# A virtual clock reckons the load of Gelu's table and longer loads of rows: a long convolution beside a gated MLP on one core

## The chip, the cores and the metric

The kernel runs on one core of a Trainium2 chip. The metric is the device time of one execution in microseconds; less is better. The number compared is the median of several runs.

## The reference

Everything is float32, with 2048 tokens of 576 features and a hidden width of 4608.

```python
def reference(A_u, ...):
    x = A_u
    xn = _layernorm(x, axis=-1)
    s = _A_ref(xn, ...)        # S4D: per feature a kernel of 2048 taps, K = 2 Re sum_n C exp(A dt l);
                               # y = irfft(rfft(xn) * rfft(K)) + xn * D_skip
    g = _silu(_B_ref(xn, ...)) # layernorm -> w1 + b1 -> tanh-approximated gelu -> w2 + b2
    return x + s * g
```

## The kernel before

The work on TensorE has two parts. The first is the MLP. It runs in 48 half-slots, counted from 0; each takes 3 x 128 hidden features (a group of `NG` = 12) and 512 of the tokens. A half-slot has three blocks of the first layer (L619, 14 matmuls each, 512 columns), and then eight units of the second layer (L682, 72 matmuls of 288 columns), which add to four row blocks j of the accumulator. Numbers are split into a high and a low part, so each hidden block passes through three steps: ScalarE's gelu (L655), ScalarE's copy to the high part `hh` (L658), VectorE's subtraction to the low part `hl` (L661). The first matmul that reads the third low part stands 18 matmuls and a bit behind the end of the third block. VectorE adds each finished row block to `acc` (L692). Weights are split the same way (L572 on ScalarE, L569 on VectorE).

The second part is the long convolution, in six chunks of 96 features. It is laid as "scan work" between the MLP's blocks on TensorE, in the two PSUM tiles named `cv`: table products (L996), first transforms (L1108, L1139), a second one (L1167), inverses (L1210, L1236). Its tables come from sines. For each of 36 table blocks VectorE forms phases (L917, L920), ScalarE rounds them (L923), VectorE takes the fraction (L926), ScalarE folds it (L929) and takes two sines (L934, L936), and VectorE weighs them by magnitudes (L942 forms the magnitudes; L951, L953, L955, L957 weigh). ScalarE holds one table at a time: gelu's and sine's differ, and plain copies run under either.

At the end the three factors are joined. For the first eight token blocks a combine loads rows of u, s and g into three of four `row` buffers (`combine_load`, L721 to L723, on GpSimd's queue), multiplies and adds on VectorE (L729, L730) and stores (L733). The other eight are finished behind the last two half-slots: ScalarE's tanh or silu (L765), VectorE's products and sum (L770, L772, L776, L780), and stores (L782).

The order in which all this is issued is fixed when the program is recorded. A class `Order` keeps a virtual clock for each engine and reckons a duration for each step (`act`, `dve` and the like). Between two units of TensorE, `advance` records every step of the side lines that is ready before TensorE's clock and that would end before the next step with a due time ("soon", in which gelus, low parts and additions stand) would have to begin. `take` adds 1.28 for a table load whenever a step's table isn't the current one. Ahead of a second-layer unit, `force` records the earliest startable steps, whatever they are, until that unit's inputs are recorded. A None step is a wait on the clock alone; in `end_line` one of 10 us stands for the landing of a combine's rows. `end_line` is started in half-slot 38 and its eleven combines follow each other: eight after the fourth chunk's rows are stored, and three after the last chunk's.

Of the kernel before, what the change touches and what calls it, by code (L numbers as in the profile page):

```python
# [19 lines left out]
NT = 16  # L20
# [19 lines left out]
def dve(n):  # L40
    return 0.075 + 0.00104 * n
# [10 lines left out]
class Order:  # L52
# [85 lines left out]
    def advance(self, horizon):  # L138
        while True:
            best = None  # L140
            soon = dict(self.next)
            for u in self.urgent:
                st = u[1][0]
                k = (max(u[0], self.t[st["eng"]]), 0)
                if u[0] <= horizon and (best is None or k < best[0]):
                    best = (k, u, None)
                for st in u[1]:
                    soon[st["eng"]] = min(soon.get(st["eng"], 1e9), st["by"])
            for x in self.lines:
                if x["steps"] and x["steps"][0]["by"] < 1e9:  # L150
                    st = x["steps"][0]
                    soon[st["eng"]] = min(soon.get(st["eng"], 1e9), max(st["by"], self.t[st["eng"]] + st["dur"]))
            for n, x in enumerate(self.lines):
                h = self.head(x)
                if h is None or h[0]["eng"] == "PE":
                    continue
                st, r = h
                if st["eng"] is None:
                    k = (max(r, 0), 1 + n)
                    if r > horizon:  # L160
                        continue
                else:
                    e = st["eng"]
                    b = max(self.t[e], r)
                    d = st["dur"]
                    if st["tbl"]:
                        d += 1.28 * (1 + (st["tbl"] != self.tbl))
                    if b > horizon or b + d > soon.get(e, 1e9) + st["late"]:
                        continue
                    k = (b, 1 + n)  # L170
                if best is None or k < best[0]:
                    best = (k, None, x)
            if best is None:
                break
            if best[1] is not None:
                self.go(best[1])
            else:
                self.run(best[2])
            self.pin()
# [26 lines left out]
def step(eng, dur, fn, need=(), mark=None, cv=0, at=0.0, late=0.0, tbl=None, by=1e9):  # L206
    return dict(eng=eng, dur=dur, fn=fn, need=tuple(need), mark=mark, cv=cv, at=at, late=late, tbl=tbl, by=by)
# [3 lines left out]
def mixer_kernel(ctx, tc, u, log_a_real, a_imag, c_real, c_imag, log_dt, d_skip, w1, b1, w2, b2,  # L211
# [506 lines left out]
    def combine_load(b, n, c0, c1):  # L718
        m = c1 - c0
        r = [sb.tile([P, D], F32, name="row", bufs=NROW)[:, :n * m].rearrange("p (i d) -> p i d", i=n) for _ in range(3)]  # L720
        nc.gpsimd.dma_start(r[0], u_s[:, b:b + n, c0:c1])  # L721
        nc.gpsimd.dma_start(r[1], s_s[:, b:b + n, c0:c1])
        nc.gpsimd.dma_start(r[2], g_s[b:b + n, :, c0:c1].rearrange("i p d -> p i d"))  # L723
        XS[b] = r

    def combine(b, n, c0, c1):

        x, s, g = XS[b]
        nc.vector.tensor_mul(s, s, g)  # L729
        nc.vector.tensor_add(x, x, s)  # L730
        for i in range(n):
            for y, o in enumerate(rows_at(out, b + i, c0, c1)):
                nc.gpsimd.dma_start(o, x[64 * y:64 * y + 64, i])  # L733
# [19 lines left out]
    def finish(b, c0, c1, silu, second_queue, z=None):  # L753

        c = slice(c0, c1)
        z = acc[:, b - 8, c] if z is None else z
        n = c1 - c0
        T = []

        def act_z():  # L760
            if n < D:
                T.append(sb.tile([P, TB], F32, name="h32", bufs=2)[:, :n])
            else:
                T.append(sb.tile([P, D], F32, name="row", bufs=NROW))
            nc.scalar.activation(T[0], z, AF.Silu if silu else AF.Tanh, scale=1.0 if silu else 0.5)  # L765

        def mul():
            s = XS[b][1][:, c]
            if silu:
                nc.vector.scalar_tensor_tensor(s, s, 2.0, T[0], op0=OP.mult, op1=OP.mult)  # L770
            else:
                nc.vector.tensor_mul(s, s, z)  # L772

        def mul2():
            s = XS[b][1][:, c]
            nc.vector.scalar_tensor_tensor(s, T[0], 1.0, s, op0=OP.add, op1=OP.mult)  # L776

        def total():
            x, s = XS[b]
            nc.vector.tensor_add(x[:, c], x[:, c], s[:, c])  # L780
            for y, o in enumerate(rows_at(out, b, c.start, c.stop)):
                (second_queue if y else nc.sync).dma_start(o, x[64 * y:64 * y + 64, c])  # L782
        st = [step("ACT", act(n), act_z, tbl="silu" if silu else "gelu"), step("DVE", dve(n), mul)]
        if not silu:
            st.append(step("DVE", dve(n), mul2))
        return st + [step("DVE", dve(n), total)]
# [485 lines left out]
    el, wl2, wl, nl2, pl, pl2, nl, ml, ml2, xl, wx, c3, c2, c1, c4, kl, tl, sl, vl, gl, odl, fl = [od.line() for _ in range(22)]  # L1272
# [181 lines left out]
    def wmark(n, which):  # L1454

        per = KB + 1 + G
        a = n * per + (0 if which == 1 else KB + 1)
        return [("w", k) for k in range(a, a + (KB + 1 if which == 1 else G))]
# [23 lines left out]
    for k in range(8):  # L1482
        gl["steps"].append(step("POOL", 0.7, lambda k=k: part.update({k: load_f2(k)}), mark=("f2", k),
                                need=[("f2c", k - 2)] if k > 1 else ["turns"]))
        fl["steps"].append(step(None, 4.5, lambda: None, need=[("f2", k)]))
        for f in range(2):
            fl["steps"].append(step("ACT", act(256), lambda k=k, f=f: part[k](f), mark=("f2c", k) if f else None,
                                    need=[("f2s", k - 1)] if k and k % 2 == 0 else []))
# [26 lines left out]
    def end_line():  # L1515
        for c, c0, c1, sets in ((NCH - 3, 0, CE, [(b, 1) for b in range(8)]), (NCH - 1, CE, D, [(0, 3), (3, 3), (6, 2)])):
            for b, n in sets:
                a = (b, n, c0, c1)
                ml["steps"].append(step(None, 10.0, lambda a=a: combine_load(*a), need=[("st", c), ("u", NT - 1)]))
                ml["steps"].append(step("DVE", 2 * dve(n * (c1 - c0)), lambda a=a: combine(*a)))  # L1520
                ml["steps"].append(step(None, 4.0, lambda: None))

# [46 lines left out]
    later(mid - 2, G, lambda: (parts_in(0), turn_in(1)))  # L1569
    later(mid - 1, G, lambda: parts_in(1))  # L1570
    later(NSLOT - 10, 4, end_line)
    later(NSLOT - 2, 0, lambda: wx["steps"].append(step(None, 0.0, load_identity)))
    for k in range(8):
# [40 lines left out]
    for slot in range(NSLOT):  # L1614
# [5 lines left out]
        for pos in range(NPOS):  # L1620
            if pos < G:
                need = wmark(n, 1) + [("x", tb)]
# [25 lines left out]
            else:  # L1648
                j, terms, last, hid = l2_terms(pos - G)
                need = [wmark(n, 2)[i] for i in hid] + [("h", slot, i) for i in hid]  # L1650
# [17 lines left out]
                elif last:  # L1668
                    add = cell[0]
                    chain = [step("DVE", dve(D), lambda: add(0, 2), mark=("acc", slot, j), by=add_by(pos, j))]  # L1670
                    if final:
                        x = el if slot < NSLOT - 1 else od.line()
                        st = finish(b, 0, D, slot == NSLOT - 1, nc.gpsimd if slot == NSLOT - 1 and j > 1 else nc.sync)
# [69 lines left out]
```

## Time and profile before

| | |
|---|---|
| time, median of 3 runs | 1102.57 us (1101.76 to 1102.64) |
| time of the profiled execution | 1102.84 us |
| its span | 1101.0 us, mean TensorE clock 0.999 |
| TensorE, VectorE, ScalarE, GpSimd busy | 99%, 81%, 66%, 17% |
| matmuls recorded | 11445 |
| table loads before a gelu (L655) | 39 |

"L682" is line 682 of the kernel. In the chain and the timelines the first number is the start in microseconds from the beginning of the span and the second the length. A row of waits gives the engine and its instruction, what it waited for, the sum, how often, and the longest. A row of a group of instructions gives busy time and mean nanoseconds of one, and then the idle time of the engine just ahead of them.

### The profile page before, as it was taken

What the parts mean: (1) busy time and instruction counts of PE and PEld (TensorE: products, weight loads), DVE (VectorE), ACT (ScalarE), POOL (GpSimd) and SP (SyncE); (2) the same over time, 40 slices, a digit from 0 to 9 for tenths busy, and PEclk for the clock granted to TensorE, in tenths of its full rate; (3) what the DMA queues carried; (4) which work ended last, traced back from release to release, by engine and by line L of the source; (5) the groups of instructions that cost most, each with busy time, mean ns of one, the idle gap of its engine ahead of it and who ended that gap; (6) DMA issues with size and microseconds to landing.
All of it is one profiled execution on the core that took longest, in us unless ns stands there. A gap on an engine that the chain in (4) does not pass through costs nothing.

```text
span 1101.0 us, 27023 instructions
## 1 busy us (share of the span) xinstructions
PE 1090.1 (99%) x11445; PEld 954.5 (87%) x11445; DVE 892.8 (81%) x1298; ACT 725.7 (66%) x1109; POOL 184.1 (17%) x255
## 2 busy tenths in 40 slices
PE   9999999999999999999999999999999999999997
PEld 7989899898888898888888888888888888888897
DVE  7798677979888889889997988988798986666356
ACT  6585699876848685586947669577666766335233
POOL 4566201071110100001100010000100012110320
PEclk9999999999999999999999999999999999999999
DMA  8846755745542333344723334242333425563543
GB/s 227 236 147 152 236 160 193 214 87 150 160 147 75 67 97 95 99 103 128 169 58 90 85 89 100 53 119 64 92 76 91 146 64 163 131 179 100 161 129 87
DMA packets 139649, 138.22 MB, mean 126 GB/s; under 512 B 88952, under 2 KB 105016, under 8 KB 138952
## 3 DMA queue, kind: packets, MB, share of 16 engines
q1 hardware_dynamic: 124664, 85.49, 29.7%
q0 software_dynamic: 14384, 50.27, 14.7%
q8 instruction: 89, 1.46, 0.6%
q10 hardware_dynamic: 480, 0.74, 0.3%
q14 instruction: 32, 0.26, 0.1%
HBM read 102.17 MB, written 36.63 MB: 126 GB/s over the span
## 4 chain that ended last, share of the span: by engine, by line
PE 87%; DVE 4%; ACT 3%; DMA 2%; SPq 2%; issue 1%; POOL 0%; ACTq 0%; DVEq 0%; POOLq 0%
PE mxb L682 19%; PE mxa L682 19%; PE mxb L619 18%; PE mxa L619 18%; PE cv L1167 3%; PE cv L996 3%; PE cv L1210 2%; PE cv L1139 1%; PE cv L1108 1%; PE cv L1236 1%; SPq L810 1%; DMA row<-g_s 1%; DMA w<-in_A_u_dram 1%; SPq L385 1%; ACT h L655 0%
## 5 line engine op out<-in xcount | busy, mean ns | idle before, releaser
L661 DVE TENSOR_TENSOR hl<-h,hh 128x512 fp32r<-128x512 f32 x144 | 98.7, 688 | 104.1 <-ACT hh L658 103.8
L682 PE MATMUL mxa<-w2h,hh 128*128 128x288 f32 x573 | 171.2, 299 | 2.0 <-DVE acc L692 1.0
L682 PE MATMUL mxb<-w2h,hh 128*128 128x288 f32 x576 | 171.3, 297 | 0.0
L682 PE MATMUL mxb<-w2h,hl 128*128 128x288 f32 x576 | 170.6, 296 | 0.6 <-DVE hl L661 0.5
L682 PE MATMUL mxa<-w2h,hl 128*128 128x288 f32 x573 | 169.2, 295 | 0.4 <-DVE hl L661 0.4
L682 PE MATMUL mxb<-w2l,hh 128*128 128x288 f32 x576 | 169.5, 294 | 0.0
L682 PE MATMUL mxa<-w2l,hh 128*128 128x288 f32 x573 | 168.6, 294 | 0.0
L682 PEld LDWEIGHTS mxa<-w2h,hh 128*128 128x128 f32 x573 | 107.6, 188 | 9.8 <-issue 4.2
L655 ACT ACTIVATE h<-mxa,b1t 128x512 f32<-128x512 f32 x73 | 50.1, 687 | 94.8 <-PE mxa L619 93.6
L682 PEld LDWEIGHTS mxb<-w2h,hh 128*128 128x128 f32 x576 | 108.1, 188 | 4.9 <-issue 1.8
L682 PEld LDWEIGHTS mxb<-w2h,hl 128*128 128x128 f32 x576 | 108.1, 188 | 1.6 <-DVE hl L661 1.5
L682 PEld LDWEIGHTS mxb<-w2l,hh 128*128 128x128 f32 x576 | 108.2, 188 | 0.7
L682 PEld LDWEIGHTS mxa<-w2l,hh 128*128 128x128 f32 x573 | 107.6, 188 | 0.6
L682 PEld LDWEIGHTS mxa<-w2h,hl 128*128 128x128 f32 x573 | 107.5, 188 | 0.6 <-DVE hl L661 0.6
L692 DVE TENSOR_TENSOR acc<-mxa,acc 128x576 f32<-128x576 f32 x87 | 65.3, 751 | 36.4 <-PE mxa L682 36.2
L898 POOL DMA_DIRECT2D par<-par_s x36 | 27.5, 765 | 394.6 <-DVE mg L942 317.9
L658 ACT ACTIVATE hh<-h 128x512 fp32r<-128x512 f32 x144 | 90.8, 631 | 3.7
L655 ACT ACTIVATE h<-mxb,b1t 128x512 f32<-128x512 f32 x71 | 48.8, 687 | 65.3 <-PE mxb L619 62.7
L692 DVE TENSOR_TENSOR acc<-mxb,acc 128x576 f32<-128x576 f32 x88 | 66.1, 751 | 19.5 <-PE mxb L682 19.3
L619 PE MATMUL mxa<-XH,w1h 128*128 128x512 f32 x284 | 78.3, 398 | 0.0
L619 PE MATMUL mxb<-XH,w1h 128*128 128x512 f32 x280 | 77.9, 400 | 0.0
L619 PE MATMUL mxa<-XL,w1h 128*128 128x512 f32 x284 | 76.1, 390 | 0.0
(266 smaller groups left out, 2481.5 us busy)
## 6 DMA issues: line engine op xcount, KB each, us to landing
raw<-in_B_w_dram SPq DMA_DIRECT2D x72, 288.0 KB, 3.5
raw<-in_B_w_dram SPq DMA_DIRECT2D x96, 192.0 KB, 3.5
par_s<-A POOLq DMA_DIRECT2D x4, 2160.0 KB, 9.0
par<-par_s POOLq DMA_DIRECT2D x36, 240.0 KB, 3.7
f2t<-f2q SPq DMA_DIRECT2D x24, 256.0 KB, 3.3
g2t<-g2p SPq DMA_DIRECT2D x24, 256.0 KB, 3.8
bias<-XR SPq DMA_DIRECT2D x42, 128.0 KB, 3.5
raw<-in_B_w_dram SPq DMA_DIRECT2D x48, 96.0 KB, 3.6
```

The source lines that it names most:

```text
L385: queue.dma_start(XT[b], tok(u, b))
L619: nc.tensor.matmul(q, a, b, start=j == 0 and i not in BEGUN, stop=j == len(ops) - 1, skip_group_check=True)
L655: nc.scalar.activation(t, q, AF.Gelu_apprx_tanh, bias=b1t[:, k:k + 1], scale=1.0)
L658: LAST[0] = nc.scalar.activation(hh[:, i], t, AF.Copy)
L661: nc.vector.tensor_sub(hl[:, i], t, hh[:, i].bitcast(F32))
L682: nc.tensor.matmul(q[:, dh, :288], a[:, i, c], b[:, i, d], start=i == 0 and k == 0 and not alone, stop=i == G - 1 and k == 2)
L692: nc.vector.tensor_add(o, q[:, dh:dh + n, :288], b)
L810: nc.sync.dma_start(r[32 * g:32 * g + 32].rearrange("c (b n) -> c b n", n=32), dram(src[k], 32 * g, [[N, 32], [32 * N, D // 32], [1, 32]]))
L898: nc.gpsimd.dma_start(PAR[b].rearrange("p (g i) k -> p g (i k)", g=4), dram(par_s, (b // 3 * 48 + b % 3 * 4) * NPAR, [[D * NPAR, P], [12 * ...
L996: nc.tensor.matmul(q[32 * g:32 * g + 32, i // 2, i % 2 * 64:i % 2 * 64 + 64], U[:, ri, 4 * g + i, :], v[:, ri, 4 * g + i, :], start=ri == ...
L1167: nc.tensor.matmul(Q[i][32 * q:32 * q + 32, f, ri::2], m[r, 4 * i + q, 32 * ri:32 * ri + 32], A2[r, 4 * p + 2 * i + q // 2, :, :, q % 2], ...
L1210: nc.tensor.matmul(QI[q // 2][64 * f:64 * f + 64, q % 2, i], MAT["g2t", p + i // 2][r, i % 2, f, ri], YS[p + i // 2][0][r, i % 2, ri, f], ...
```

## The change

Two reckonings of the virtual clock change; no instruction of the kernel is rewritten, but the recorded order may be another.

```diff
@@ Order.advance
                     d = st["dur"]
                     if st["tbl"]:
                         d += 1.28 * (1 + (st["tbl"] != self.tbl))
+                    elif e == "ACT" and self.tbl != "gelu":
+                        d += 1.28
                     if b > horizon or b + d > soon.get(e, 1e9) + st["late"]:
                         continue
@@ end_line
-                ml["steps"].append(step(None, 10.0, lambda a=a: combine_load(*a), need=[("st", c), ("u", NT - 1)]))
+                ml["steps"].append(step(None, 13.0, lambda a=a: combine_load(*a), need=[("st", c), ("u", NT - 1)]))
                 ml["steps"].append(step("DVE", 2 * dve(n * (c1 - c0)), lambda a=a: combine(*a)))
                 ml["steps"].append(step(None, 4.0, lambda: None))
```

The first makes `advance` test a ScalarE step that needs no table as if it were 1.28 us longer while another table than gelu's is loaded; the clock itself is advanced by the step's own duration as before. The second lets a combine's VectorE steps be recorded 3 us later after its loads.

## The prediction

> **What bounds the kernel now.** I read the page's first part, then what TensorE waited for, then the chain that ended last in time order, and only then ScalarE's and VectorE's rows at the places where the chain leaves TensorE.
>
> ```profile
> PE 1090.1 (99%) x11445; PEld 954.5 (87%) x11445; DVE 892.8 (81%) x1298; ACT 725.7 (66%) x1109; POOL 184.1 (17%) x255
> engine line waited for: us in total, times, longest us
> PE mxa L682 <- DVE acc L692: 1.0, 1, 1.0
> PE mxb L682 <- DVE hl L661: 0.5, 2, 0.3
> PE mxa L682 <- ACT h L655: 0.5, 2, 0.2
> PE mxa L682 <- issue: 0.4, 1, 0.4
> PE mxa L682 <- DVE hl L661: 0.4, 1, 0.4
> ```
>
> TensorE is busy for 99% of the span. The change neither adds nor removes a matmul, so all that it can win is waiting time of TensorE, and the rows show what kind there is: the second layer (L682) waits for a gelu (L655), for a low part (L661) behind a gelu, for an addition (L692), once for nothing that the profile shows. These rows count only time with nothing in flight; matmuls overlap, so the true loss at a place is larger, and I measure it along the chain instead, between equal sets of blocks.
>
> ```profile
> 706.37 3.17 PE mxb L619 x14
> 709.54 1.03 PE cv L996 x64
> 710.58 1.53 PE cv L1167 x56
> 712.11 3.40 PE mxa L619 x14
> 715.50 1.59 PE mxb L682 x12
> 717.09 0.79 PE mxa L682 x6
> 720.27 2.38 PE mxb L682 x18
> 725.02 0.43 PE mxb L602 x2
> 728.02 3.18 PE mxb L619 x13
> 734.37 2.94 PE mxb L619 x13
> ```
>
> ```profile
> 327.55 3.19 PE mxb L619 x14
> 342.30 2.38 PE mxb L682 x18
> 469.85 3.19 PE mxb L619 x14
> 484.75 2.38 PE mxb L682 x18
> 923.19 8.23 DMA row<-g_s
> ```
>
> From the end of the L619 block at 709.54 to the x18 block at 720.27 lie 10.73 us: a table product (L996), a stage of the scan (L1167), the third first-layer block and 36 second-layer matmuls, undisturbed. The same set after 327.55 + 3.19 = 330.74 takes until 342.30, that is 11.56, so 0.83 are lost; after 469.85 + 3.19 = 473.04 until 484.75 it takes 11.71, so 0.98 are lost. These are the two clearest places that the table rule aims at.
>
> **What one such place consists of.** ScalarE there:
>
> ```profile
> 332.13 1.28 ACT L934 ACT_TABLE_LOAD   x1
> 333.43 1.18 ACT L934 ACTIVATE w<-w,tv 128x1040 f32<-128x1040 f32 x1
> 335.36 1.10 ACT L923 ACTIVATE w<-w 128x1040 int32<-128x1040 f32 x1
> 336.47 1.28 ACT L655 ACT_TABLE_LOAD   x1
> 337.77 0.69 ACT L655 ACTIVATE h<-mxa,b1t 128x512 f32<-128x512 f32 x1
> ```
>
> Between the second and the third gelu of a half-slot stand a sine under its own table, three short copies, and then a step without a table, L923, that was let in because the virtual clock forgot the load that must follow. The third gelu's input is done at 330.74 + 1.03 + 1.53 + 3.40 = 336.70; the gelu starts at 337.77, 1.07 late.
>
> **The change part by part.** The change acts through the order in which each engine's instructions are issued; that order of the changed program can be listed without running it, and I compare it with the one before.
>
> The table rule at the two places: in half-slot 15 L923 now stands behind the gelu; without its 336.47 - 335.36 = 1.11 the gelu can start at 336.66, before its input at 336.70. The 0.83 go. What is late next is nothing: VectorE has the four steps ahead of the low part done before that gelu ends. The place at 473 and a third of the kind near 668 (load, half a sine, one copy, load) are gone from the order altogether. The third I set at 0.7, between nothing and the 0.98 of its larger sister. Removed: 0.83 + 0.98 + 0.7 = 2.5.
>
> The other waits: the addition's 1.0 comes from two transposes and a split of the scan that VectorE ran ahead of it in half-slot 24; in the new order they fall into the next half-slot, so 1.0 goes, plus about 0.1 in flight. The 0.4 for a low part belongs to a combine (L729) that stood ahead of it and waited for rows of g: the landing took 8.23 us, while the clock reckons 10 from a moment that the queue reached late. With 13 the combines stand some 3 us further behind their loads, and none stands ahead of a low part with less than that; The row's 0.4 is the least that goes; with what lay in flight it is up to 0.7 (at the two places above, losses of 0.83 and 0.98 stand against idle times of at most 0.3 and 0.2 each), and I take 0.6. The 0.4 of no visible cause need not come again; I count 0.3 of it. Together 2.5 + 1.1 + 0.6 + 0.3 = 4.5 removed, 3.4 at the least and 4.9 at the most. The waits of the first 300 us stay, as both orders are equal there.
>
> Cost at nothing: the order has 73 table loads between gelu and sine instead of 69, four times 1.28 = 5.1 us, which ScalarE's idle third hides; without that cover they would cost up to 5.1. TensorE's insertions of scan work into the two layers are 78 in both orders; one costs about 3.40 - 3.17 = 0.2, and the number is equal. Bias pairs (L602) fall from 15 to 11. With a pair a half-slot has 0.43 + 3.18 + 2.94 = 6.55 for what costs 3.40 + 3.17 = 6.57 without: no price.
>
> What is added. First, half-slot 32, at about 735 us. ScalarE has there, after the second gelu, load, second half of a sine (L936), load, third gelu; VectorE has the whole weighing chain that needs this sine, and the next magnitudes, ahead of the third low part.
>
> ```profile
> L661 DVE TENSOR_TENSOR hl<-h,hh 128x512 fp32r<-128x512 f32 x144 | 98.7, 688 | 104.1 <-ACT hh L658 103.8
> L936 ACT ACTIVATE w<-w 128x1040 f32<-128x1040 f32 x36 | 39.1, 1086 | 0.1
> L942 DVE TENSOR_TENSOR mg<-par 128x1024 f32<-128x1024 f32 x36 | 44.0, 1221 | 0.7
> L951 DVE TENSOR_TENSOR w<-w,mg 128x1024 f32<-128x1024 f32 x36 | 43.8, 1216 | 1.6 <-ACT w L936 1.6
> L953 DVE TENSOR_TENSOR w<-w,mg 128x1024 f32<-128x1024 f32 x36 | 43.7, 1213 | 0.0
> L957 DVE SCALAR_TENSOR_TENSOR w<-w,mg 128x512 f32<-128x512 f32 x36 | 24.5, 682 | 0.0
> L955 DVE TENSOR_TENSOR w<-w,mg 128x512 f32<-128x512 f32 x36 | 24.5, 681 | 0.0
> ```
>
> Counted from the end of the second first-layer block: the sine starts 333.43 - 330.74 = 2.69 later and ends at 2.69 + 1.09 = 3.78. VectorE's chain is 1.22 + 1.21 + 0.68 + 0.68 + 1.22 = 5.01, or 4.7 if neighbours overlap by some 0.07, which is my estimate. The low part then ends at 3.78 + 4.7 to 5.0 + 0.69 = 9.2 to 9.5. TensorE wants it after 1.53 + 3.40 + 1.59 + 0.79 + 0.3 = 7.6 (L1167, third block, 18 matmuls, two more). It waits 1.6 to 1.9; I take 1.8. No deadline prevents this, since the forced recording in front of a second-layer unit takes whatever starts earliest.
>
> Second, half-slots 19 and 20: VectorE has five steps of the same kind between the second and third low part, and the third comes out 0 to 0.5 late in each; I take 0.5 for both. Third, waits that I don't see: every one of some 35 reordered half-slots can hold one, none to 2 in all; I take 0.5.
>
> Fourth, the tail.
>
> ```profile
> L729 DVE TENSOR_TENSOR row<-row 128x384 f32<-128x384 f32 x9 | 4.9, 549 | 2.0 <-DMA row<-g_s 2.0
> L730 DVE TENSOR_TENSOR row<-row 128x384 f32<-128x384 f32 x9 | 5.0, 558 | 0.3
> 1096.57 0.46 DVE w L780
> 1056.02 3.18 POOL L733 DMA_DIRECT2D out_dram<-row  x6 [10.77 <-DVE row L730]
> out_dram<-row POOLq DMA_DIRECT2D x16, 48.0 KB, 2.2
> 1084.48 0.69 ACT L655 ACTIVATE h<-mxa,b1t 128x512 f32<-128x512 f32 x1 [1.24 <-PE mxa L619]
> ```
>
> Before, VectorE's last finish steps end the kernel at 1096.57 + 0.46. The last chunk's inverse now stands some 16 us later, each combine has 3 us more, and so the last combine (128x384, L729 and L730) lands inside this closing chain, between the two halves of the last block: 0.55 + 0.56 = 1.1 on the path. It would cost nothing only if VectorE idled there, which it does not.
>
> Sum against the profiled execution's own 1102.84 (span 1101.0 and 1.8 around it): 1102.84 - 4.5 + 1.8 + 0.5 + 0.5 + 1.1 = 1102.2. The median of the runs shown, 1102.57, is 0.27 lower than that execution, so I forecast 1102.0 for the median.
>
> [...] In the rows above the gelu starts at 337.77, 1.30 after the load's start at 336.47, so a switch costs 1.3 here. [...]
>
> **The rivals.** *Faster:* the old waits go and the new ones are fewer: nothing unseen, half-slots 19 and 20 on time, the most removed. That gives 1102.57 - 4.9 + 1.8 + 1.1 = 1100.6, and below 1100.4 if the chain of half-slot 32 costs a little less. For it speaks that the order shows no other sine between a second and third gelu with VectorE's weighing ahead; against it, that the tail's 1.1 stands on the end itself.
>
> *Slower:* the last gelu is held by row buffers. In the last half-slot a finish step on ScalarE stands ahead of the third gelu and takes the row buffer that the last combine but one stores from. By VectorE's order and the durations above that combine ends near 1077.8, my estimate; its six stores take 3.18 to issue, to 1081, and 2.2 to land, so the buffer is free at 1083.2, the step is over by 1083.9, and the gelu's input comes at 1084.48. It decides from a landing of about 3 us; each further us is 1 us of the kernel, and with the 8.23 that a landing took elsewhere it is 5 us, 1107. For it: three combines and the last loads crowd there. Against: the stores are small and their median is short.
>
> *Nothing:* old and new waits cancel closer than I reckon, 1102.6; this lies within my forecast.
>
> **How the numbers follow.** What counts as no change is 0.2%, 2.2 us, about what a measurement of this kernel can tell: 1100.4 to 1104.8. Forecast with its neighbour "nothing" 0.67; faster rival 0.17; slower rival, with half-slot 32 at its upper bound and 2 us of unseen waits on its side, 0.16. The range: below, everything at its cheap end, 1102.57 - 4.9 + 1.6 + 1.1 = 1100.4, and 0.3 under it, 1100.1; above, removed only 3.4, added 1.9 + 1.0 + 2.0 + 1.1 = 6.0, which is 1105.2; all of it together is rare and I stop at 1104.5.
>
> **What would show it.** In the changed profile: no gelu more than 0.3 late in half-slot 15; a wait of L682 for L661 of 1.5 or more near 735, the longest of the run; no idle of L729 for g inside the second layer; L729 and L730 between the two last L770 steps, and the closing chain 1.1 longer. The forecast is wrong if the wait near 735 is missing, if TensorE's waits sum to more than 6 us after 300 us, or if the third gelu of the last half-slot waits for a store.

## The result, and the profile after

The changed kernel is slower: 1108.40 us (1108.23 to 1108.65) beside 1102.29 for the kernel before in the same series, a ratio of 1.0056, 95% interval 1.0042 to 1.0070. The forecast was 1102.0 with 1100.1 to 1104.5, so it lies outside the range, by 3.9 us.

From line 167 on, the changed kernel's line numbers are two higher than before's: L682 is L684, L661 is L663, L1076 is L1078. The experiments below keep before's numbers, up to two lines off in the two that move weight loads (syncE_order and all_mended).

The page of the changed kernel, first part, and the rows of what TensorE waited for that are used here (three of 0.4 and 0.5 are left out):

```profile
PE 1090.5 (99%) x11445; PEld 954.6 (86%) x11445; DVE 890.8 (81%) x1298; ACT 730.5 (66%) x1113; POOL 183.9 (17%) x255
PE mxa L684 <- DVE hl L663: 1.9, 2, 1.7
PE mxa L1300 <- POOL XL L1293: 1.3, 1, 1.3
PE mxb L684 <- DVE hl L663: 1.3, 2, 1.0
PE mxa L684 <- ACT hh L660: 0.6, 1, 0.6
PE mxa L684 <- ACT h L657: 0.4, 1, 0.4
PE cv L1110 <- ACT pr L1087: 0.4, 1, 0.4
PE mxb L684 <- DVE acc L694: 0.4, 1, 0.4
```

TensorE still does the same 11445 matmuls in the same busy time. What changed is what it waits for: the addition's 1.0 and the 0.4 without a cause are gone, and low parts (L663) now hold it for 3.2 in four places, where they held it for 0.9 in three. (The 1.3 for XL belongs to the start.)

These rows count only time with nothing in flight. Measured as the prediction did, between equal sets of blocks along the chain, the losses over the undisturbed sets are, in us:

| place | before | changed |
|---|---|---|
| 336 / 457 / 478 to 482 / 668 to 671 (gelu's table late) | 0.72 / 0.15 / 0.90 / 0.60 | 0 |
| 550 (addition) | 1.15 | 0 |
| 739 (no visible cause) | 0.49 | 0 |
| 932 (low part behind a combine) | 0.63 | 0 |
| 453 (half-slot 20) | 0 | 0.24 |
| 481, 643 (additions late) | 0 | 0.52, 0.26 |
| 525 (half-slot 23, third low part) | 0 | 1.31 |
| 682 to 686 (second gelu behind a copy of xc) | 0 | 2.00 |
| 738 (half-slot 32, third low part) | 0 | 2.00 |
| 827 to 836 (the same copy, next chunk) | 0 | 1.35 |
| 1089 (last third gelu) | 0 | 0.54 |
| closing chain | 0 | 2.10 |
| sum | 4.64 | 10.32 |

At 336 and 478 the prediction had 0.83 and 0.98, against one undisturbed set. The difference of the sums, 5.7, is close to the 5.4 by which the two profiled spans differ (1106.4 and 1101.0); the start, where both orders are equal, took 0.38 less in the changed kernel's execution (half-slot 15's first block begins at 323.98, for 324.36).

The largest place that the prediction didn't have is at 682. First ScalarE's timeline, then SyncE's queue at the same time (start, length, instruction, and in brackets the idle time ahead and what ended it):

```profile
671.27 2.10 ACT L1078 ACTIVATE xt<-xc 128x768 f32<-128x768 f32 x1
676.00 1.28 ACT L657 ACT_TABLE_LOAD   x1
677.29 0.69 ACT L657 ACTIVATE h<-mxb,b1t 128x512 f32<-128x512 f32 x1
679.18 0.39 ACT L1003 ACTIVATE kt<-cv 128x256 f32<-128x256 f32 x1 [0.54 <-PE cv L998]
683.38 2.11 ACT L1078 ACTIVATE xt<-xc 128x768 f32<-128x768 f32 x1 [3.82 <-DMA xc<-xn_s]
685.40 0.67 ACT L657 ACTIVATE h<-mxa,b1t 128x512 f32<-128x512 f32 x1
```

```profile
667.20 2.40 SPq L539 DMA_DIRECT2D raw<-in_B_w_dram  x3
676.56 0.33 SPq L541 DMA_DIRECT2D raw<-in_B_w_dram  x1
676.93 3.88 SPq L1043 DMA_DIRECT2D xc<-xn_s  x4
```

ScalarE copies a chunk of xc in two halves through one buffer. The first half's copy ends at 673.37, so the second load could go from there. It issues at 676.93, because on SyncE's queue it stands behind a load of raw weights whose buffer comes free at 676.5; it lands after 683.3. ScalarE idles 3.82 in front of that copy, and the half-slot's second gelu (685.40) is queued behind it, though its block was done at 682.5; the third (688.20) follows late. Before, the same two steps look like this, ScalarE first and then SyncE:

```profile
656.63 1.09 ACT L923 ACTIVATE w<-w 128x1040 int32<-128x1040 f32 x1 [1.88 <-DVE w L920]
657.63 2.10 ACT L1076 ACTIVATE xt<-xc 128x768 f32<-128x768 f32 x1
659.76 0.85 ACT L1085 ACTIVATE pr<-xt 128x768 fp32r<-128x768 f32 x1
660.62 1.28 ACT L655 ACT_TABLE_LOAD   x1
```

```profile
659.75 2.46 SPq L1041 DMA_DIRECT2D xc<-xn_s  x4
672.59 2.40 SPq L537 DMA_DIRECT2D raw<-in_B_w_dram  x3
```

Before, the copy of the first half ran under the sine's table just ahead of a gelu's load; that is the kind of step that the new rule holds back. It now comes 13.6 us later, the load that it releases is 17 us later on SyncE's queue, and there a raw load is ahead of it.

The closing chain of the changed kernel, VectorE and then GpSimd's queue:

```profile
1098.57 0.45 DVE L772 SCALAR_TENSOR_TENSOR A<-A,h 128x288 f32<-128x288 f32 x1
1098.94 0.55 DVE L731 TENSOR_TENSOR row<-row 128x384 f32<-128x384 f32 x1
1099.53 0.56 DVE L732 TENSOR_TENSOR row<-row 128x384 f32<-128x384 f32 x1
1100.86 0.46 DVE L782 TENSOR_TENSOR w<-w,A 128x288 f32<-128x288 f32 x1
1100.38 2.10 POOL L735 DMA_DIRECT2D out_dram<-row  x4 [0.87 <-DVE row L732]
```

The last combine does stand between two finish steps. Behind it GpSimd issues four stores until 1102.48, after VectorE's end at 1101.32; the span ends 5.1 after VectorE's last step, for 4.0 before.

### The profile page after: what moved, and what is told of

Read it like the earlier page. It is cut to its first block, busy times and chain, and to the rows that moved or that the text cites. A ratio compares the mean times of both kernels' runs of the same rounds, so it can differ in the third digit from the quotient of the medians.

```text
span 1106.4 us, 27035 instructions
## 1 busy us (share of the span) xinstructions
PE 1090.5 (99%) x11445; PEld 954.6 (86%) x11445; DVE 890.8 (81%) x1298; ACT 730.5 (66%) x1113; POOL 183.9 (17%) x255
## 4 chain that ended last, share of the span: by engine, by line
PE 87%; DVE 4%; ACT 3%; DMA 2%; issue 2%; SPq 1%; POOL 0%; POOLq 0%; DVEq 0%; ACTq 0%
PE mxb L684 19%; PE mxa L621 19%; PE mxa L684 19%; PE mxb L621 18%; PE cv L1169 3%; PE cv L998 3%; PE cv L1212 2%; PE cv L1141 1%; PE cv L1238 1%; PE cv L1110 1%; DMA xc<-xn_s 1%; SPq L1043 1%; DVE acc L694 1%; DMA acc<-in_A_u_dram 0%; DVE w L953 0%
## 5 line engine op out<-in xcount | busy, mean ns | idle before, releaser
L663 DVE TENSOR_TENSOR hl<-h,hh 128x512 fp32r<-128x512 f32 x144 | 98.8, 688 | 115.9 <-ACT hh L660 115.7
L684 PE MATMUL mxa<-w2h,hh 128*128 128x288 f32 x573 | 170.9, 298 | 1.2 <-ACT hh L660 0.6
L684 PE MATMUL mxb<-w2h,hh 128*128 128x288 f32 x576 | 171.6, 298 | 0.4 <-DVE acc L694 0.4
L684 PE MATMUL mxb<-w2h,hl 128*128 128x288 f32 x576 | 170.2, 295 | 1.3 <-DVE hl L663 1.3
L684 PE MATMUL mxa<-w2h,hl 128*128 128x288 f32 x573 | 169.4, 296 | 1.9 <-DVE hl L663 1.9
L684 PE MATMUL mxb<-w2l,hh 128*128 128x288 f32 x576 | 169.5, 294 | 0.0
L684 PE MATMUL mxa<-w2l,hh 128*128 128x288 f32 x573 | 168.7, 294 | 0.0
L684 PEld LDWEIGHTS mxa<-w2h,hh 128*128 128x128 f32 x573 | 107.6, 188 | 7.0 <-issue 2.1
L684 PEld LDWEIGHTS mxb<-w2h,hh 128*128 128x128 f32 x576 | 108.1, 188 | 5.7 <-issue 1.7
L684 PEld LDWEIGHTS mxa<-w2h,hl 128*128 128x128 f32 x573 | 107.5, 188 | 2.6 <-DVE hl L663 2.6
L684 PEld LDWEIGHTS mxb<-w2h,hl 128*128 128x128 f32 x576 | 108.1, 188 | 1.8 <-DVE hl L663 1.8
L684 PEld LDWEIGHTS mxb<-w2l,hh 128*128 128x128 f32 x576 | 108.2, 188 | 0.7
L684 PEld LDWEIGHTS mxa<-w2l,hh 128*128 128x128 f32 x573 | 107.6, 188 | 0.7
```

The source lines that it names most:

```text
L663: nc.vector.tensor_sub(hl[:, i], t, hh[:, i].bitcast(F32))
L684: nc.tensor.matmul(q[:, dh, :288], a[:, i, c], b[:, i, d], start=i == 0 and k == 0 and not alone, stop=i == G - 1 and k == 2)
```

## The experiments

Theory A, from this reading: the losses are made by the order that the table rule records before 915 us (xc behind raw loads, VectorE's table work ahead of low parts), and 2 us by the 13.0 in the tail. Theory B: the 13.0 is to blame. Theory C: it is the four further table loads themselves.

### Each half of the change alone, the tail alone, and a load of xc

table_only has the rule and 10.0; lead13_only the 13.0 without the rule. late_lead10 and chunk_load_gpsimd start from the changed kernel:

```diff
  late_lead10
- step(None, 13.0, lambda a=a: combine_load(*a), ...
+ step(None, 13.0 if c < NCH - 1 else 10.0, lambda a=a: combine_load(*a), ...
  chunk_load_gpsimd, in load(i)
- nc.sync.dma_start(XC[i][...], ...
+ (nc.sync if i or not c else nc.gpsimd).dma_start(XC[i][...], ...
```

> The changed kernel with the combines' lead put back to 10.0: the table rule alone. Theory A (what the changed kernel lost lies in the order that the table rule records before 915 us: chunk loads that land late at 682 and 827, 3.5 us; VectorE work ahead of the third low part at 525 and 738, 3.3 us; against some 4 us of old waits that are gone), and 2 us in the closing chain from the 13.0: this kernel keeps the losses before 915 us and is rid of the closing combine: 1106.0 to 1107.0, with the same two waits of ScalarE for xc. Theory B (the 13.0 is to blame, and before 915 us the table rule's gains and losses cancel): 1102. Theory C (each further load of a table costs its 1.28 us: 77 loads here, 73 in the changed kernel, 69 before): 1108.4 + 4 x 1.28 = 1113.5.

> The kernel before with the combines' lead at 13.0 and without the table rule: its order differs from before's only after some 915 us, and no combine stands in the closing chain. Theory A: the waits before 915 us are before's, the 0.6 us wait behind a combine near 932 is gone: 1101.5 to 1102.3. Theory B (the 13.0 costs whatever stands ahead of it): 1104 to 1106. Theory C (69 loads as before): 1102.

> The changed kernel with 13.0 for the first eight sets of combines and 10.0 for the last three: on TensorE and SyncE nothing is moved, on VectorE the last combine goes ahead of the last half-slot's additions. Theory A: the 2.1 us of the closing chain go (1.06 of the two combine steps, 1.0 of GpSimd's stores that ended last), the order before is that of the changed kernel: 1106.0 to 1106.6. If the closing chain were hidden (its combine not on the path): 1108.4. The combine brought forward may hold an addition for its loads of rows: up to 1 us given back.

> The changed kernel with the first load of xc of each chunk but the first issued on GpSimd's queue in place of SyncE's; nothing else is moved on TensorE, ScalarE or VectorE. On SyncE's queue the loads at 676.9 and 821.3 stand behind a load of raw weights that waits for its buffer; on GpSimd's they stand behind loads of par that are long issued. Theory A: ScalarE's two waits for xc (3.82 and about 3.15 us) go, and TensorE's waits of 2.0 and 1.5 us at 682 and 827 with them: 1104.6 to 1105.2. Theory C (the loads of tables hold the gelus there, the copy would be as late without the wait): 1108.4. If half of it comes back because the chunk's steps then run earlier into the same VectorE work: 1106.5.

Measured in one series, the kernel before at 1102.47:

| kernel | us | ratio to before (95%) |
|---|---|---|
| table_only | 1107.05 | 1.0046 (1.0034 to 1.0058) |
| lead13_only | 1102.65 | 1.0004 (0.9996 to 1.0013) |
| late_lead10 | 1106.58 | 1.0038 (1.0025 to 1.0050) |
| chunk_load_gpsimd | 1112.69 | 1.0094 (1.0081 to 1.0107) |

The table rule alone loses about 5 us, the 13.0 alone nothing that can be told: theory B falls. Table_only has 77 loads and is no slower than the changed kernel with 73; beside late_lead10, which has 73 and is without the tail's loss too, it is 0.9 us slower and not 5.1. So theory C falls too. In table_only's profile the places 481, 525, 643, 682, 738 and 827 are those of the changed kernel within 0.1, but for 481 (1.45 for 0.52; it lies between those two in the other kernels with this order) and 827 (0.90 for 1.35). In lead13_only's, before's places are back and the one at 932 is gone; its last combine stands at 1078.5, ahead of the last half-slot's second gelu, and not in the tail. So the closing combine needs both edits: the 13.0 and the later last chunk that the rule makes. With late_lead10 the tail's 2.1 and the 0.54 at 1089 are gone.

chunk_load_gpsimd went the wrong way, and for reasons of its own. I had moved the wrong load: ScalarE idles before the copy of the second half, and I had taken it for the first. The wait stayed:

```profile
683.66 2.12 ACT L1076 ACTIVATE xt<-xc 128x768 f32<-128x768 f32 x1 [4.10 <-DMA xc<-xn_s]
```

And TensorE's work ended only 0.6 us later than in the changed kernel, but the span 3.0 later. GpSimd's drain (the row DRAIN of its queue) at the program's end had grown, to 6.41 us from 3.95. TensorE also lost 1.6 from 689 on to a halved clock (last section). That led to the next four.

### The right load, the low parts, all together, and the drain

```diff
  second_chunk_load, in load(i)
+ (nc.gpsimd if i and c in (3, 4) else nc.sync).dma_start(XC[i][...], ...
  third_low_first: half-slot 23 and 32, order on VectorE alone
  23: ... L917 L920 [L661] L953 L955 -L661-
  32: ... L951 L953 [L661] L955 L957 L942 -L661-
  all_three: late_lead10 + second_chunk_load + third_low_first
  before_first_loads, on the kernel before
+ (nc.sync if i or not c else nc.gpsimd).dma_start(XC[i][...], ...
```

> The changed kernel with the second load of xc of the fourth and fifth chunk (the ones that ScalarE waited for at 679 and 824) issued on GpSimd's queue; TensorE, ScalarE and VectorE keep their order. The run before this moved the first loads, which were not the late ones. On SyncE's queue the second load stands behind a load of raw weights and issues at 676.9; its buffer is free from 673.4, when the copy of the first load ends (671.27 + 2.10). On GpSimd's queue it issues from 673.4 on, 3.1 us for four, and lands about 3.1 us later, at 679.7, when ScalarE comes to the copy at 679.6. Theory A: ScalarE's waits of 3.8 and 3.1 us shrink to under 1, TensorE's excess at 682 to 686 (2.0) and 827 to 831 (1.1) goes: 1104.9 to 1105.6, and up to 1 us more if GpSimd's closing drain grows with the number of its transfers (6.4 us with 20 more, 3.95 in the changed kernel). If the landing is as late from this queue: 1108.4.

> The changed kernel with the third low part of the half-slots at 525 and 738 put ahead of two (525) and three (738) VectorE steps of the tables; every other instruction keeps its place on every engine, and the virtual clock is not changed. The low part then starts when its high part ends, 524.45 for 525.97 and 737.6 for 739.67. Theory A: TensorE's waits of 1.31 and 2.0 us there go, and nothing else is late, since VectorE does the same work by the same time: 1108.4 - 3.3 = 1105.1 (1104.9 to 1105.6). If the waits are only handed on (TensorE, earlier by 2 us, then waits for the additions behind the tables' steps): 1106.5 to 1108.4.

> The changed kernel with the three edits together: 10.0 for the last three sets of combines, the second loads of xc of the fourth and fifth chunk on GpSimd's queue, the third low part first at 525 and 738. If the losses are separate (theory A): 1108.4 - 2.0 (closing chain, last gelu) - 3.1 - 3.3 = 1100.0, to 1101.0 with a longer closing drain of GpSimd, and faster than before by 1.5 to 2.5 us. If TensorE's waits are handed from one place to the next: 1103 to 1106.

> The kernel before with the first load of xc of each chunk but the first on GpSimd's queue (20 transfers more on that queue, as in the run that moved them in the changed kernel, and came out 4.3 us above it while TensorE's work ended only 0.6 us later). None of before's loads of xc is waited for, so the order's waits stay: if GpSimd's closing drain grows with the transfers that its queue has carried, 1102.4 + 2.4 = 1104.5 to 1105.5, with a drain of some 6.4 us for 4.2; if that run's drain had its own cause (the combine's stores in the closing chain), 1102.4.

The kernel before took 1103.01 in this series.

| kernel | us | ratio to before (95%) |
|---|---|---|
| second_chunk_load | 1108.03 | 1.0048 (1.0036 to 1.0060) |
| third_low_first | 1110.38 | 1.0062 (1.0050 to 1.0074) |
| all_three | 1105.61 | 1.0025 (1.0017 to 1.0034) |
| before_first_loads | 1105.97 | 1.0027 (1.0013 to 1.0041) |

second_chunk_load: at 682 ScalarE's wait fell as reckoned, from 3.82 to 0.53, and TensorE's loss with it, to nothing. At 827 it fell from 3.15 to 2.38 only, and of the 1.35 there 0.58 stayed.

```profile
674.17 3.13 POOL L1041 DMA_DIRECT2D xc<-xn_s  x4 [12.15 <-ACT xt L1076]
680.60 2.11 ACT L1076 ACTIVATE xt<-xc 128x768 f32<-128x768 f32 x1 [0.53 <-DMA xc<-xn_s]
```

Most of that gain is given back by the drain. The rows give, for GpSimd's queue at the program's last line, the shortest, median and longest drain in ns. second_chunk_load, with 237 transfers on that queue:

```profile
L1739 POOLq DRAIN  x3: 46/103/6167, 1099.1 to 1105.8; - x3
```

The changed kernel, with 229:

```profile
L1741 POOLq DRAIN  x3: 46/103/3952, 1101.7 to 1106.2; - x3
```

before_first_loads, with 249:

```profile
L1739 POOLq DRAIN  x3: 46/103/6509, 1096.3 to 1103.4; - x3
```

The kernel before, with 229:

```profile
L1739 POOLq DRAIN  x3: 46/103/4178, 1095.6 to 1100.8; - x3
```

The longest grows by 2.2 us with 8 further transfers and by 2.3 with 20 (6.41 in chunk_load_gpsimd; 5.94 in all_three, with 8 more), so not in proportion to their number.

third_low_first was a miss for theory A. The wait at 738 went, and TensorE met another behind it (VectorE's timeline, and the row of what TensorE waited for between 730 and 750):

```profile
738.60 0.69 DVE L661 TENSOR_TENSOR hl<-h,hh 128x512 fp32r<-128x512 f32 x1 [0.31 <-ACT hh L658]
739.21 0.69 DVE L955 TENSOR_TENSOR w<-w,mg 128x512 f32<-128x512 f32 x1
739.81 0.69 DVE L957 SCALAR_TENSOR_TENSOR w<-w,mg 128x512 f32<-128x512 f32 x1
740.53 1.23 DVE L942 TENSOR_TENSOR mg<-par 128x1024 f32<-128x1024 f32 x1
741.67 0.95 DVE L1184 TENSOR_TENSOR pr<-cv,kk 128x768 f32<-128x768 f32 x1
742.66 0.56 DVE L1190 TENSOR_TENSOR ys<-pr 128x384 f32<-128x384 f32 x1
743.13 0.75 DVE L692 TENSOR_TENSOR acc<-mxa,acc 128x576 f32<-128x576 f32 x1
```

```profile
PE mxa L682 <- DVE acc L692: 2.1, 1, 2.1
```

With what lay in flight 2.3 are lost there, and 1.6 more to the clock right behind (last section). VectorE works without a gap from 738.6 to 745. As long as the tables' steps stand ahead of the additions (L692), these come when the sum of the work is done. At 525 it was the same: 1.31 became 1.04 for an addition and 0.28 behind it. Its five executions split by the clock: the two with a mean granted clock of 0.998 and 0.999 took 1108.34 and 1108.77, as long as the changed kernel, and the three with 0.996 and 0.997 took 1110.38 to 1110.96. all_three was built on that edit and kept this loss; it was some 4.5 us above its expectation.

### A swap on SyncE's queue, and the tables' steps behind the additions

```diff
  syncE_order: at two places, SyncE's queue alone
- raw x1, xc x4, raw x3
+ xc x4, raw x1, raw x3
  tables_behind: half-slot 23 and 32, VectorE alone
  23: L661 ... L692 ... L692 [L953 L955]
  32: L661 L1184 L1190 L692 L692 [L955 L957 L942 L942]
  all_mended: late_lead10 + syncE_order + tables_behind
```

> The changed kernel with one swap on SyncE's queue at two places: the second load of xc of the fourth and fifth chunk goes ahead of the load of raw weights behind which it stood; no other instruction moves on any engine and GpSimd's queue carries what it carried. The load can issue from 673.4 (its buffer is free) for 676.9, the raw load follows at 677 as before. Theory A: as in the run that put these loads on GpSimd's queue, TensorE's waits at 682 to 686 and 827 to 831 go (3.0 us there), and the closing drain stays at 3.95 us: 1108.4 - 3.0 = 1105.4 (1105.0 to 1105.9). If the longer drain of the two runs before had to do with when the loads land and not with their queue, it stays long here: 1107.6.

> The changed kernel with two (525) and four (738) VectorE steps of the tables put behind the half-slot's second addition instead of ahead of the third low part; nothing else moves. The run that put the low part first, but left these steps ahead of the additions, only handed the wait on (2.0 us at 738 became 3.9 at 740 to 744, 1.31 at 525 became 1.32 at 527). Theory A2 (VectorE is the bound for some 10 us there; the wait goes if its work that is not due moves to where it idles, 1.5 us before 748 and more after): 1.3 + 2.0 us less: 1105.1 (1104.8 to 1106.0). If VectorE has no room within the half-slot, the steps wait is handed to the next additions or to the tables' own matmuls: 1107 to 1110.

> The changed kernel with the swap on SyncE's queue, the tables' steps behind the additions, and 10.0 for the last three sets of combines. If the losses are separate: 1108.4 - 3.0 - 3.3 - 2.0 = 1100.1 (1099.6 to 1101.0), 1.5 to 3 us faster than before, with a closing drain of 3.95 to 4.2 us. If TensorE's waits are handed on: 1103 to 1106.

The kernel before took 1101.31 in this series.

| kernel | us | ratio to before (95%) |
|---|---|---|
| syncE_order | 1106.15 | 1.0037 (1.0023 to 1.0050) |
| tables_behind | 1106.48 | 1.0046 (1.0034 to 1.0059) |
| all_mended | 1100.33 | 0.9990 (0.9981 to 0.9999) |

syncE_order: the loads issue at 674.57, ScalarE doesn't idle in front of the copy, and the losses at 682 and 827 (3.35) are gone; the drain is 3.99, for 6.17 in second_chunk_load, which has the same loads on GpSimd's queue. So in these runs the drain follows the queue that carries the loads, not the time at which they land. The time fell by 2 us and not by 3; in its profiled execution, the longest of its five, 1.55 were lost again at 740, to the clock (below). Its two executions with a mean clock of 0.998 and 0.999 took 1103.96 and 1105.48, the three with 0.997 1106.15 to 1107.45.

tables_behind: at 738 the wait is gone (0.23 and 0.36 at the next places remain of 2.0). At 525 1.03 of 1.31 came back at 530 and 0.3 more at 545, because VectorE has next to no idle time there to put the work into: 0.3 us from 524 to 544. The edit is worth 1.1 us.

all_mended: what TensorE waited for, the whole list:

```profile
PE mxa L1298 <- POOL XL L1291: 1.3, 1, 1.3
PE mxb L619 <- DVE acc L692: 0.9, 1, 0.9
PE cv L502 <- DVE row L442: 0.4, 1, 0.4
PE mxb L682 <- DVE acc L692: 0.4, 1, 0.4
PE mxa L634 <- ACT XH L506: 0.4, 1, 0.4
```

From the changed kernel's 1.0056 to 0.9990 is 7.3 us. The three edits alone, by their ratios, are worth 2.0, 2.1 and 1.1, together 5.2; the intervals of single ratios are 1.3 to 1.5 us to each side. By the blocks and the closing chain, all_mended's profile is rid of some 7.8, so 7.3 is about what the places themselves amount to; what the single runs fall short by may be chance, and in syncE_order it is also the halved clock, which all_mended's profile doesn't have. all_mended is the fastest of all, but by 0.1% over the kernel before, which is less than a measurement of this kernel can tell.

## Why the prediction was wrong, point by point

**The removed waits, 4.5: right.** All the named places went, 4.64 by the blocks. Each part was near: the table places 2.4 (0.15 of it at 457, a place that wasn't named) for 2.5 reckoned, the addition 1.15 for 1.1, the combine 0.63 for 0.6, the one without a cause 0.49 for 0.3.

**Half-slot 32, 1.8: right.** 2.0 were lost, and in the predicted way. The chain from the sine to the low part:

```profile
733.80 1.10 ACT w L938
734.93 1.23 DVE w L953
738.52 0.04 DVE mg L944
739.67 0.69 DVE hl L663
740.41 0.80 PE mxa L684 x4
```

But the reason given, that `force` takes whatever starts earliest, was half of it: third_low_first shows that putting the low part first only moves the wait to the additions, and tables_behind that it goes when the tables' steps stand behind these. What held TensorE was that VectorE had this work ahead of both.

**Half-slots 19 and 20, 0.5:** 0.24, at 453.

**Waits that I don't see, 0.5 ("none to 2 in all"): this step failed.** The additions came to 10.3 by the blocks, for 3.9 in the sum, and 4.9 of the 6.4 between are this term; the tail has 1.0 and the last gelu 0.54. The unseen waits were 5.4: 2.00 and 1.35 for xc, 1.31 in half-slot 23, 0.52 and 0.26 for additions. The xc waits are the larger part, and they were to be had: the steps that the rule holds back were followed on ScalarE and VectorE, and not with the load that one of them releases, nor on SyncE's queue that this load is moved past. syncE_order shows it: undoing this queue's order alone takes the whole 3.35 away. Half-slot 23 is of the kind that I had priced in half-slot 32 and had half priced in 19 and 20; I listed half-slots with a sine between gelus and passed over one where VectorE alone was late.

**The tail, 1.1: a term mis-sized.** The combine landed where it was predicted, and its two steps cost 1.06. Its four stores, which GpSimd issues behind it, I left out; they end after VectorE does and cost another 1.0.

**The slower rival came true besides, at its low price.** The row buffer was waited for:

```profile
1081.32 3.18 POOL L735 DMA_DIRECT2D out_dram<-row  x6 [12.11 <-DVE row L732]
1087.19 0.69 ACT L767 ACTIVATE row<-acc 128x576 f32<-128x576 f32 x1 [1.77 <-DMA out_dram<-row]
1087.78 0.67 ACT L657 ACTIVATE h<-mxa,b1t 128x512 f32<-128x512 f32 x1
```

The combine's stores began at 1081.3 and not at 1077.8; as TensorE ran some 2.8 us later there than before, that is 0.8 later than reckoned against it. They landed 2.7 after the issue, for 2.2 reckoned, and 0.54 were lost. The two signs of a wrong forecast that this profile gave were that one and the sum of waits, 8.2 by the blocks between 300 us and the closing chain.

**The price of a switch.** The gelu starts 1.29 after its load's start here (676.00 and 677.29), for 1.30 before; the load's own row is 1.28 long in both.

## What to carry to other kernels

When a rule holds a step back, follow it with everything that it releases: the load that it frees a buffer for moves to another place in its own queue, and what stands ahead of it there decides, here over the 3.35 us at 682 and 827. A wait on a loaded engine was not mended here by putting its late step first; at 738 it went when work that wasn't due moved to where the engine idles, and at 525, where it hardly idles, it came back. A sum in which known gains stand against "waits that I don't see" needs for these a price from how many places are reordered: here some 35 reordered half-slots held 5.4 us, more than the waits that were aimed at.

## What the runs showed of the hardware that was not expected

GpSimd's closing drain, above: about 4 us with 229 transfers on its queue, 5.9 to 6.5 with 8 or 20 more, for two choices of the loads that were moved, and back to 4 when loads at the same places left from SyncE. It stands at the end of the program: the time from TensorE's last matmul to the end of the span grew by 2.2 in second_chunk_load and, in before_first_loads, by 1.8 of the drain's 2.3. Why 8 transfers cost about as much as 20 stays open.

In four of these traces a wait of TensorE cost more than its length. In syncE_order (stretch; length; PE busy; ...; granted clock, third from the end):

```profile
738.00:740.00 2.00, 0.65 (x5) 0.65 (x6) 2.00 (x3) 0.00 (x0) 0.00 (x0) 1.00 0.00 0
740.00:742.00 2.00, 2.00 (x12) 2.00 (x11) 1.97 (x4) 0.71 (x2) 0.00 (x0) 0.57 0.00 0
742.00:744.00 2.00, 2.00 (x11) 2.00 (x10) 1.16 (x3) 0.00 (x0) 0.00 (x0) 0.58 0.00 0
744.00:746.00 2.00, 2.00 (x41) 1.84 (x43) 1.33 (x3) 0.00 (x0) 0.00 (x0) 1.00 0.00 0
```

TensorE idles for 1.74 us from 737.6 on. Behind that its granted clock is 0.50 for 3.4 us, reckoned from the 0.57 and 0.58 above, 2 x (0.43 + 0.42) / 0.50, and 1.55 us are lost. By the same reckoning it was 0.50 for 3.4 us behind gaps of 2.13 us in third_low_first and all_three, and behind 1.47 us of idle spread over 685 to 689 in chunk_load_gpsimd. It stayed at 1.00 behind gaps of 1.72 to 1.73 us between 737 and 742 in the changed kernel, table_only, late_lead10, second_chunk_load and chunk_load_gpsimd. As the ends of matmuls are modelled, 1.73 and 1.74 can't be told apart, and 1.47 is less than either: what decided whether the clock fell, these traces don't show.
